# All eight heads in a loop on TensorE and VectorE, wo loaded whole behind V, and a part of the MLP weights on eight DMA engines

## The chip, the cores and the metric

The kernel runs on one core of a Trainium2 chip. All numbers are float32. The metric is device time in microseconds (us) of one execution; the reference point is the median of three runs of the kernel before.

## The reference

One decode step of a gated block, for a batch of 8 with one token each and a model width of 512:

```
xn = layernorm(x)                                    # x: (8, 1, 512)
q  = xn @ wq                                         # 32 query heads of 128
s  = softmax(q k^T / sqrt(128)) v, joined, @ wo      # 8 key/value heads, 4096 positions
z  = gelu(xn @ w_in);  z1, z2 = halves of 896
z2 = layernorm(z2);    g = w_sp * z2 + b_sp          # sequence length 1: two scalars
out = x + s * silu((z1 * g) @ w_out)
```

Every key/value head serves 4 query heads. Each of the two caches holds 8 x 8 x 4096 x 128 numbers, 134 MB. wq and wo are 8 MiB each, w_in and w_out together 5376 KB.

## The kernel before

**Layout and stream.** The host lays out the caches so that, for one head and one half of the batch (4 of 8), the keys or the values are one array of 128 partitions x 16384 columns (8 MiB, `SLOT` columns). SBUF has three such slots, A, B and C. SyncE (SP) issues all large loads, in this order: wq into B, the MLP weights into C, and then for every head h: K's first half into A (called K0 below, `load_k`, L547), K's second half into B (K1), V's first half into C (V0, `load_v`, L553), V's second half into B (V1). Each load waits until TensorE has read what lay in its slot before.

**Compute.** First come the layer norm, the projection of q (`project_q`) and the MLP branch (`mlp`), whose result is the tile `gate`. Then, per head (`head`):

- `spread_q` (L499): VectorE copies the head's q into `qz`, the left operand of the scores.
- `scores` (L506): 32 matmuls per half, q against K, into the PSUM tile `sc`.
- `softmax` (L510 to L529): VectorE takes the maximum, ScalarE the exponential, TensorE and VectorE put sums and maxima of the 4 column groups together and transpose the probabilities.
- `values` (L538 to L541): for each batch entry 8 matmuls with V, then a product and a reduction on VectorE.
- `combine` (L544): a small matmul for each batch entry; the one of entry b stands behind the values of entry b+1.
- L606: VectorE copies the result `po` into `oT`, or, for late heads, into `oT_end`.

Float32 matmuls count as two records each in the profile, transposes as one.

**wo.** There are 32 row blocks m of wo (4 per head), of 128 x 512. Blocks below `FOLDED` (24) are applied in `folded_wo` (L566), 8 output rows in each of four column groups, summed in one PSUM bank; that sum is copied out by VectorE (L620) and put into the final layout by 8 small matmuls (L625). The other blocks go through `direct_wo` (L574), 8 small matmuls each, straight into the final layout. L625 stands between the direct blocks, at `FOLD_AT` (29). Then VectorE multiplies by the gate, adds x (L630, L631), and SP stores the result (L632).

**The last head.** Heads 0 to 6 are a hardware loop on TensorE (`LOOPED`); all other engines' programs, and TensorE's last head, stand singly, instruction behind instruction. In the last head V0 goes into A, 12 blocks of wo (3072 KB) into C, then V1 in two halves of 4096 KB into B, then the other 20 blocks in pieces of 8, 5, 3, 2, 1 and 1 blocks. `folded_wo` of blocks 0 to 11 stands ahead of V1's values, that of 12 to 19 ahead of the last combine, that of 20 to 23 behind it.

**Order and waits.** Nothing is scheduled: the `Recorder` keeps each engine's instructions in the order of the source. `plan` derives the waits from overlapping tile regions and leaves out those that follow from others; `emit_op` writes them. In the loop, TensorE waits for VectorE through a counting semaphore `token`, taken down by one at each use; the large loads have one semaphore for each slot, taken down by 16.

Of the kernel before, what the change touches and what calls it, by code (L numbers as in the profile page):

```python
# [30 lines left out]
WO_EARLY = 12  # L31
WO_LATE = [(WO_EARLY, 20), (20, 25), (25, 28), (28, 30), (30, 31), (31, 32)]
FOLDED = 24
FOLD_AT = 29
LOOPED = HKV - 1
# [44 lines left out]
class Op:  # L80
    def __init__(self, eng, name, args, kw, line):
        self.eng, self.name, self.args, self.kw, self.line = eng, name, args, kw, line
        self.reads, self.writes = [], []
        self.waits = []
        self.sem = None
        self.iter = None
        self.pos = None


class Recorder:  # L90
# [5 lines left out]

    NAMES = ["tensor", "vector", "scalar", "gpsimd", "sync"]

    def __init__(self, nc):
        self.nc = nc  # L100
        self.ops = []
        self.touched = {}
        self.now = None
        self.rounds = 0
        self.order = {n: [] for n in self.NAMES}
        self.dma_sems = {}
        for n in self.NAMES:
            setattr(self, n, Proxy(self, n))
# [8 lines left out]

    def add(self, eng, name, args, kw):
# [5 lines left out]
        op.dma = name == "dma_start"  # L124
        op.key = key
        vals = list(args) + list(kw.values())
        aps = [v for v in vals if isinstance(v, bass.AP)]
# [8 lines left out]
        if eng == "gpsimd" and name == "affine_select":  # L136
            op.reads += op.writes
# [3 lines left out]
        op.at = len(self.order[eng])  # L141
        self.order[eng].append(op)
        op.n = len(self.ops)
        self.ops.append(op)
        op.deps = set()
# [15 lines left out]
    def meet(self, eng):  # L161

        op = Op(eng, "meet", (), {}, 0)
        op.dma, op.key = False, None
        op.deps = {self.order[n][-1] for n in self.NAMES if n != eng and n != "sync" and self.order[n]}
        op.deps = {o for o in op.deps if not o.dma}
        op.at, op.n = len(self.order[eng]), len(self.ops)
        self.order[eng].append(op)
        self.ops.append(op)

    def plan(self):
# [5 lines left out]
        def learn(k, o):  # L177
            for t, v in o.known.items():
                k[t] = max(k.get(t, -1), v)
            k[track(o)] = max(k.get(track(o), -1), o.at)  # L180

        for op in self.ops:
            k = know[op.eng]
            for o in sorted(op.deps, key=lambda o: -o.n):
                if k.get(track(o), -1) < o.at:
                    op.waits.append(o)
                    learn(k, o)
            op.known = dict(k)

        body = [op for op in self.order["tensor"] if op.iter is not None]  # L190
        size = len(body) // self.rounds
        rounds = [body[i * size:(i + 1) * size] for i in range(self.rounds)]
        place = {(o.eng, o.iter, o.pos): o for o in self.ops if o.iter is not None}
        for p in range(size):
            need = set()
            for i, ops in enumerate(rounds):
                assert ops[p].pos == p and ops[p].name == ops[0 * size + p].name
                for o in ops[p].waits:
                    assert o.iter == i, (ops[p].line, ops[p].name, i, o.eng, o.line, o.iter)
                    need.add((o.eng, o.pos))  # L200
            for i, ops in enumerate(rounds):
                ops[p].waits = [place[e, i, q] for e, q in sorted(need)]
        takes = [o.pos for op in rounds[0] for o in op.waits if not o.dma]
        assert takes == sorted(set(takes)), takes
        assert all(o.dma or o.eng == "vector" for op in rounds[0] for o in op.waits)

        for op in self.ops:
            op.token = op.counted = False
        for op in self.ops:
            for o in op.waits:  # L210
                if o.dma:
                    continue
                if op.eng == "tensor" and op.iter is not None:
                    o.token = True
                else:
                    o.counted = True
        for p in range(size):
            any_ = any(ops[p].counted for ops in rounds)
            for ops in rounds:
                ops[p].counted = any_  # L220

        nc = self.nc
        self.first = None
        self.sems = {}

        def sem(name):
            if name not in self.sems:
                self.sems[name] = nc.alloc_semaphore(name)
            return self.sems[name]

        for n in self.NAMES:
            c = 0
            for op in self.order[n]:
                if op.dma:
                    op.sem = sem(op.key or f"dma{op.n}")
                    op.taken = op.key is not None
                    continue
                if op.token and op.counted:
                    c += 1
                elif op.counted:  # L240
                    c += 1
                op.level = c
            sem(n)
        sem("token")

    def emit_op(self, op):
        nc = self.nc
        eng = getattr(nc, op.eng)
        with nc.source_location(__file__, op.line, op.name):
            waits = []  # L250
            for o in sorted(op.waits, key=lambda o: o.n):
                if o.dma:
                    if o.taken:
                        assert op.eng == "tensor"
                        eng.wait_ge(o.sem, 16).then_inc(o.sem, -16)
                    else:
                        waits.append((o.sem, 16))
                elif op.eng == "tensor" and op.iter is not None:
                    t = self.sems["token"]
                    eng.wait_ge(t, 1).then_inc(t, -1)  # L260
                else:
                    waits.append((self.sems[o.eng], o.level))
            for s, v in waits:
                eng.wait_ge(s, v)
# [3 lines left out]
            if op.dma:  # L268
                ins.then_inc(op.sem, 16)
            elif op.counted:  # L270
                ins.then_inc(self.sems[op.eng], 1)
                if op.token:
                    eng.wait_ge(self.sems[op.eng], op.level).then_inc(self.sems["token"], 1)
            elif op.token:
                ins.then_inc(self.sems["token"], 1)

    def emit(self):
        nc = self.nc
        self.plan()
        for n in self.NAMES[1:]:  # L280
            for op in self.order[n]:
                self.emit_op(op)
        ops = self.order["tensor"]
        inside = [i for i, op in enumerate(ops) if op.iter is not None]
        size = len(inside) // self.rounds
        for op in ops[:inside[0]]:
            self.emit_op(op)
        with nc.tensor.Fori(0, self.rounds):
            for op in ops[inside[0]:inside[0] + size]:
                self.emit_op(op)  # L290
        for op in ops[inside[-1] + 1:]:
            self.emit_op(op)
        last = self.ops[-1]
        assert last.dma and last.eng == "sync"
        nc.sync.wait_ge(last.sem, 16)
# [24 lines left out]
def gqa_gmlp_decode(real, x, kT, v, wq, wo, w_mlp, out):  # L320
# [344 lines left out]
```

## Time and profile before

| What | us |
|---|---|
| median of 3 runs (678.53 to 678.9) | 678.71 |
| the profiled execution | 678.71 |
| its span, first to last instruction | 677.3 |
| TensorE matmul busy | 375.2 |
| VectorE busy | 167.5 |
| ScalarE busy | 13.4 |

The profile shows one execution. Times in its rows are us from the start of the span, unless marked ns. PE is TensorE's matmuls, PEld its weight loads, PEldq and PEq its sequencer, DVE is VectorE, ACT ScalarE, SPq the issue queue of SyncE. L538 is line 538 of the kernel before. A row of the timeline has the start, the duration, the engine, the line, the operation, output and inputs, the number of records, and in brackets how long the engine had been idle and what ended that.

### The profile page before, as it was taken

The page shows a single profiled execution, that of the slowest core. Times are in us where ns is not written, and L with a number is a line of the kernel's source. Part 1 is how long each engine was busy: PE and PEld are TensorE (multiplying, and loading weights), DVE is VectorE, ACT ScalarE, POOL GpSimd, SP SyncE. Part 2 cuts the span into 40 slices and gives each one's busy share as a digit, 9 for nine tenths or more (in the row PEclk, how much of TensorE's full clock was granted, in tenths as well). Part 3 has the DMA queues.
Part 4 walks back from the last instruction along what each step waited for, and adds up shares of the span by engine and source line. Part 5 has one row for each costly group of instructions (what it writes and reads, how often), then busy time and mean ns, then how long its engine had stood idle before and what let it go on. Part 6 is the DMA issues. An engine that isn't in the chain of part 4 may idle for free. (4 is left out here: it accounts for less than half of the span.)

```text
span 677.3 us, 5857 instructions
## 1 busy us (share of the span) xinstructions
PE 375.2 (55%) x2658; PEld 119.5 (18%) x2658; DVE 167.5 (25%) x277; ACT 13.4 (2%) x27; POOL 2.8 (0%) x14
## 2 busy tenths in 40 slices
PE   0547554546665455456755454655654465655657
PEld 0122121112111111111211121211211121111212
DVE  2141042302430033401521024401432024400342
ACT  0000000000000000000000000000000000000000
POOL 1000000000000000000000000000000000000000
PEclk9967666878767678877766678887676678766697
DMA  8999999999999999999999999999999999999997
GB/s 373 449 434 434 433 434 433 434 433 433 433 433 433 433 433 433 434 433 433 433 433 433 433 434 433 433 433 437 437 437 437 433 437 445 433 437 434 404 423 318
DMA packets 6233, 290.90 MB, mean 429 GB/s; under 512 B 832, under 2 KB 848, under 8 KB 1360
## 3 DMA queue, kind: packets, MB, share of 16 engines
q1 hardware_dynamic: 6192, 290.75, 99.3%
q8 instruction: 7, 0.11, 0.1%
q10 hardware_dynamic: 32, 0.02, 0.0%
q14 instruction: 2, 0.02, 0.0%
HBM read 290.74 MB, written 0.03 MB: 429 GB/s over the span
## 5 line engine op out<-in xcount | busy, mean ns | idle before, releaser
L506 PE MATMUL sc<-slot_B,qz 128*32 128x512 f32 x512 | 74.4, 746 | 76.6 <-PEq L506 76.6
L538 PE MATMUL o_ps<-slot_B,tbuf 128*16 128x512 f32 x512 | 77.5, 732 | 70.5 <-PEq L538 61.6
L506 PE MATMUL sc<-slot_A,qz 128*32 128x512 f32 x512 | 74.4, 746 | 47.6 <-PEq L506 47.6
L540 DVE TENSOR_TENSOR o_all<-o_ps,diag 128x512 f32<-128x512 f32 x64 | 44.3, 691 | 161.0 <-PE o_ps L538 161.0
L538 PE MATMUL o_ps<-slot_C,tbuf 128*16 128x512 f32 x448 | 67.0, 739 | 20.5 <-PEq L538 20.5
L510 DVE TENSOR_REDUCE nm<-sc 128x1 f32<-128x1024 f32 x8 | 9.8, 1224 | 269.5 <-PE sc L506 269.5
L541 DVE TENSOR_REDUCE o_sb<-o_all 128x128 f32<-128x512 f32 x64 | 67.8, 1060 | 2.2
L506 PEld LDWEIGHTS sc<-slot_B,qz 128*32 128x32 f32 x512 | 20.4, 134 | 130.5 <-issue 130.5
L506 PEld LDWEIGHTS sc<-slot_A,qz 128*32 128x32 f32 x512 | 20.7, 133 | 94.8 <-issue 94.8
L544 PE MATMUL po<-fold,o_sb 128*128 128x4 f32 x128 | 25.6, 270 | 12.3 <-PEq L544 12.3
L544 PEld LDWEIGHTS po<-fold,o_sb 128*128 128x128 f32 x128 | 20.3, 199 | 68.5 <-issue 64.2
L538 PEld LDWEIGHTS o_ps<-slot_B,tbuf 128*16 128x16 f32 x512 | 13.4, 106 | 100.5 <-issue 90.2
L538 PEld LDWEIGHTS o_ps<-slot_C,tbuf 128*16 128x16 f32 x448 | 13.7, 112 | 57.0 <-issue 56.8
L528 PE MATMUL scr<-ident,pbuf 128*128 128x128 f32 x64 | 14.8, 409 | 10.6 <-PEq L528 9.3
L511 ACT ACTIVATE pbuf<-sc,nm 128x1024 f32<-128x1024 f32 x8 | 8.9, 1114 | 556.1 <-DVE nm L510 556.1
L528 PEld LDWEIGHTS scr<-ident,pbuf 128*128 128x128 f32 x64 | 11.8, 211 | 11.0 <-issue 9.7
L529 DVE COPY tbuf<-scr 128x512 f32<-128x512 f32 x16 | 11.1, 692 | 10.6 <-PE scr L528 10.6
L415 PE MATMUL scr<-slot_B,xnT 128*32 128x512 f32 x64 | 9.0, 713 | 8.2 <-PEq L415 8.2
L538 PE MATMUL o_ps<-slot_A,tbuf 128*16 128x512 f32 x64 | 9.8, 753 | 3.9 <-PEq L538 3.9
L514 PE MATMUL scr<-ident,nm 128*1 128x128 f32 x8 | 2.2, 269 | 11.8 <-PEq L514 10.4
L394 PE MATMUL scr<-ident,tbuf 8*128 8x8 f32 x4 | 0.6, 255 | 12.9 <-DVE tbuf L391 12.9
L521 PE MATMUL scr<-wl,same 128*128 128x1 f32 x16 | 3.5, 286 | 6.1 <-PEq L521 5.4
(102 smaller groups left out, 88.4 us busy)
## 6 DMA issues: line engine op xcount, KB each, us to landing
slot_B<-in_v SPq DMA_DIRECT2D x2, 4096.0 KB, 33.8
slot_C<-in_w_mlp SPq DMA_DIRECT2D x1, 5376.0 KB, 34.2
slot_C<-in_wo SPq DMA_DIRECT2D x1, 3072.0 KB, 35.4
slot_C<-in_wo SPq DMA_DIRECT2D x1, 2048.0 KB, 41.4
slot_C<-in_wo SPq DMA_DIRECT2D x1, 1280.0 KB, 44.0
slot_C<-in_wo SPq DMA_DIRECT2D x1, 768.0 KB, 45.4
slot_C<-in_wo SPq DMA_DIRECT2D x1, 512.0 KB, 46.1
slot_C<-in_wo SPq DMA_DIRECT2D x2, 256.0 KB, 46.4
```

What stands on the lines that cost most here:

```text
L415: nc.tensor.matmul(pq[R * g:R * (g + 1), :], xnT[:, k, :], wq_sb[:, k, lo:lo + REP * DH], start=(k == 0), stop=(k == NK - 1))
L506: nc.tensor.matmul(sc[R * g:R * (g + 1), c, :], qz[:, b * R:(b + 1) * R], k_sb[:, i, c, g, :], start=(b == 0), stop=(b == B - 1))
L510: nc.vector.tensor_reduce(nm, sc, op=ALU.max, axis=AX.XY, negate=True)
L511: nc.scalar.activation(p.rearrange("p j s -> p (j s)"), sc.rearrange("p c s -> p (c s)"), AF.Exp, bias=nm, accum_out=l)
L514: nc.tensor.transpose(a, nm, ident)
L521: nc.tensor.matmul(tot, same_all, wl, start=True, stop=True)
L528: nc.tensor.transpose(t[:, j * P:(j + 1) * P], p[:, 4 * c + j, :], ident)
L529: nc.vector.tensor_copy(pT[:, :, 4 * c:4 * c + 4].rearrange("p b j (g r) -> p (j g) b r", g=G), t.rearrange("p (m b r) -> p m b r", b=B, r ...
L538: nc.tensor.matmul(of[R * c:R * c + G * REP, :], pT[:, b, j, :], v_unit[:, j], start=(j < G), stop=(j >= J - G))
L540: nc.vector.tensor_mul(o_all[b % 2], o, diag[:, :, None].to_broadcast([P, G, DH]))
L541: nc.vector.tensor_reduce(o_sb[b % 2], o_all[b % 2].rearrange("p g d -> p d g"), op=ALU.add, axis=AX.X)
L544: nc.tensor.matmul(po[:, b * REP:(b + 1) * REP], o_sb[b % 2], fold, start=True, stop=True)
```

## The change

Five things change together.

- **Loops.** All eight heads, the last one included, are now the loop on TensorE, and VectorE's part of the heads becomes a loop of eight rounds as well. Each pair of an engine and a looping engine gets a semaphore of its own; a wait in the loop is for a fixed count within the round, and at the end of a round the looping engine takes down what the round has counted (`share`): five such waits on TensorE, three on VectorE. An engine outside the loops that waits for an instruction in a loop gets the next later point of that engine at which the instruction is known to be done (`moved`, `early`).
- **Copies.** `spread_q` and the copy of `po` go from VectorE to ScalarE.
- **wo.** In the last head V0 goes into C and V1 into B, in one piece, as in all heads. wo goes into A, where K0 lay, in seven pieces behind V1 (12, 8, 5, 3, 2, 1 and 1 blocks). All its matmuls stand behind the last head.
- **Folding.** 28 blocks instead of 24 are folded, and L625 stands behind block 29.
- **MLP weights.** The last 640 of their 10752 columns are a transfer of their own, `w_low`, whose source has 8 rows instead of 128, so that 8 DMA engines carry it.

The core of the diff:

```diff
-WO_EARLY = 12
-WO_LATE = [(WO_EARLY, 20), (20, 25), (25, 28), (28, 30), (30, 31), (31, 32)]
-FOLDED = 24
-FOLD_AT = 29
-LOOPED = HKV - 1
+WO_PARTS = [(0, 12), (12, 20), (20, 25), (25, 28), (28, 30), (30, 31), (31, 32)]
+FOLDED = 28
+FOLD_AT = 30
+LOW_E = 8
+LOW_COLS = 640
...
+    LOOPS = ["vector", "tensor"]
...
+        moved = {}
         for op in self.ops:
...
+            if self.inside(op):
+                continue
+            for d in op.waits:
+                if d.dma:
                     continue
...
+                at = d
+                if self.inside(d) and d.tokens:
+                    q = d.pos + 1
+                    while any(place[d.eng, i, q].known.get(d.eng, -1) < place[d.eng, i, d.pos].at
+                              for i in all_rounds):
+                        q += 1
+                    at = place[d.eng, d.iter, q]
+                    moved[op.n, d.n] = at
...
+            eng = getattr(nc, n)
+            with eng.Fori(0, self.rounds):
+                for op in ops[first:first + self.size[n]]:
+                    self.emit_op(op)
+                for (m, src), c in sorted(self.share.items()):
+                    if m == n:
+                        s = self.sem(src, n) if src in self.NAMES else self.sem(src)
+                        eng.wait_ge(s, c).then_inc(s, -c)
...
-    nc.sync.dma_start(slots["C"][:, :n_mlp], w_mlp, key="C")
+    n_main = n_mlp - LOW_COLS
+    nc.sync.dma_start(slots["C"][:, :n_main], w_mlp)
+    nc.sync.dma_start(slots["C"][:, n_main:n_mlp],
+                      w_low[:, :P // LOW_E * LOW_COLS].rearrange("e (i n) -> e i n", n=LOW_COLS))
...
-        nc.vector.tensor_copy(qz.rearrange("p (b s) -> p b s", b=B)[:, :, :REP], qT[:, h])
+        nc.scalar.copy(qz.rearrange("p (b s) -> p b s", b=B)[:, :, :REP], qT[:, h])
...
-        nc.sync.dma_start(slots["C"][:, lo * D:hi * D], wo[:, lo * D:hi * D])
-
-    wo_sb = slots["C"].rearrange("p (m d) -> p m d", d=D)
+        nc.sync.dma_start(slots["A"][:, lo * D:hi * D], wo[:, lo * D:hi * D])
+
+    wo_sb = slots["A"].rearrange("p (m d) -> p m d", d=D)
...
     def head(h):
-        last = h == HKV - 1
         spread_q(h)
         for half, n in enumerate("AB"):
             scores(half, load_k(h, half, n))
         softmax()
-        for half, n in enumerate("AB" if last else "CB"):
-            if last and half:
-                load_wo(0, WO_EARLY)
-                v_sb = load_v(h, half, n, 2)
-                for lo, hi in WO_LATE:
-                    load_wo(lo, hi)
-                folded_wo(0, WO_EARLY)
-            else:
-                v_sb = load_v(h, half, n)
+        for half, n in enumerate("CB"):
+            v_sb = load_v(h, half, n)
             for i in range(HALF):
                 b = half * HALF + i
                 values(b, v_sb[:, i])
                 if b > 0:
                     combine(b - 1)
-        if last:
-            folded_wo(WO_EARLY, WO_LATE[0][1])
         combine(B - 1)
...
-        nc.vector.tensor_copy(to, po.rearrange("p (b r) -> p r b", r=REP))
+        nc.scalar.copy(to, po.rearrange("p (b r) -> p r b", r=REP))
...
     nc.meet("tensor")
-    for h in range(LOOPED):
+    nc.meet("vector")
+    for h in range(HKV):
         with nc.round(h):
             head(h)
-    for h in range(LOOPED, HKV):
-        head(h)
-
-    folded_wo(WO_LATE[0][1], FOLDED)
+
+    for lo, hi in WO_PARTS:
+        load_wo(lo, hi)
+    folded_wo(0, FOLDED)
     part_sb = pbuf[:, :D]
     nc.vector.tensor_copy(part_sb, part)
     direct_wo(FOLDED, FOLD_AT)
...
-        "w_mlp": np.concatenate([
...
+        "w_mlp": c(w_mlp[:, :-LOW_COLS]),
+        "w_low": np.concatenate([w_mlp[:, -LOW_COLS:].reshape(LOW_E, -1), np.zeros((LOW_E, 64), np.float32)], axis=1),
```

216 lines of the change are left out of this document (103 added, 113 removed).

## The prediction

> **What bounds the kernel now.** I read the page first: shares, slices, queues.
>
> ```profile
> span 677.3 us, 5857 instructions
> ...
> PE 375.2 (55%) x2658; PEld 119.5 (18%) x2658; DVE 167.5 (25%) x277; ACT 13.4 (2%) x27; POOL 2.8 (0%) x14
> ...
> GB/s 373 449 434 434 433 434 433 434 433 433 433 433 433 433 433 433 434 433 433 433 433 433 433 434 433 433 433 437 437 437 437 433 437 445 433 437 434 404 423 318
> ...
> q1 hardware_dynamic: 6192, 290.75, 99.3%
> q8 instruction: 7, 0.11, 0.1%
> ```
>
> No engine is busy for more than 55%, while the 16 DMA engines are busy for 99.3% of the span and move a flat 433 GB/s. 290.75 MB at that rate take 671.5 us of 677.3. The kernel is one stream of loads; no compute in the middle can gain anything as long as the queue never runs dry. What can move is the start, the evenness of the 16 engines, and what follows the last byte. So the second view is the chain that ended last:
>
> ```profile
> 628.26 46.46 DMA slot_C<-in_wo
> 674.72 0.04 issue
> 674.76 0.47 PE sc L574 x16
> ```
>
> The last piece of wo lands at 674.72, 16 matmul records follow, and TensorE is through at 675.23. From there to the end of the span, 2.07 us, the change touches nothing. Third, the busy time of the DMA engines in the last stretch (the last three figures are granted clock, DMA share and GB/s):
>
> ```profile
> 672.50:673.00 0.50, 0.50 (x48) 0.50 (x44) 0.34 (x1) 0.00 (x0) 0.00 (x0) 1.00 0.55 217
> 673.00:673.50 0.50, 0.49 (x36) 0.33 (x25) 0.35 (x1) 0.00 (x0) 0.00 (x0) 1.00 0.43 168
> 673.50:674.00 0.50, 0.50 (x36) 0.50 (x40) 0.00 (x0) 0.00 (x0) 0.00 (x0) 1.00 0.60 209
> 674.00:674.50 0.50, 0.50 (x44) 0.44 (x32) 0.00 (x0) 0.00 (x0) 0.00 (x0) 1.00 0.14 53
> ```
>
> From 672.5 on about half of the engines have nothing left, and the other half works on for nearly two us. The work left there is (0.55 + 0.43 + 0.60 + 0.14) x 0.5 = 0.86 us of all 16 engines: perfectly even, the stream would end about 1 us earlier. That is the most that evenness is worth.
>
> **The last 640 columns on 8 engines.** The transfer is 128 x 640 x 4 B = 327,680 B: 20,480 B for each of 16 engines, or 40,960 B for each of 8. One engine moves 433/16 = 27.1 GB/s, so 8 engines get 0.76 us more than now and 8 get 0.76 us less, for the rest of the run, as the queue never empties. If the 8 late engines are the relieved ones, every landing from there on comes 0.76 us earlier (the spread of nearly 2 us exceeds twice 0.76); if they are the loaded ones, 0.76 us later. (Its rows are short, 2,560 B; the last wo pieces, with rows of 2,048 B, moved at 217/0.55 = 395 GB/s of all engines, 9% slower, which would make the loaded side 0.9 us, not the one that is then late.) No view names the engines. What makes an engine late is, as I read it, a block of instructions that it has to bring in between loads: the page has 7 of them on q8, 16 KB or about 0.6 us of one engine each. By the start times of the packets they came on engines other than the eight that carry x, and x, of 8 rows like the new transfer, should go to the same eight as that. I take -0.76 us and keep both ends.
>
> **wo whole behind V.** Bytes and order of the rest stay, so the end of the stream stays. But the second half of V now lands before all of wo instead of behind 3072 KB of it, and the 12 matmuls of wo that filled a gap, as well as the 8 between the last units, go behind the last head. So the tail has to be added up again, from these rows (start, us, engine, line, records):
>
> ```profile
> slot_C<-in_wo SPq DMA_DIRECT2D x1, 3072.0 KB, 35.4
> ...
> 191.30 0.18 PEld L538 LDWEIGHTS o_ps<-slot_B,tbuf 128*16 128x16 f32 x8 [8.92 <-issue]
> 204.33 0.36 PE L544 MATMUL po<-fold,o_sb 128*128 128x4 f32 x2 [1.64 <-PEq L544]
> 268.58 0.18 PEld L538 LDWEIGHTS o_ps<-slot_B,tbuf 128*16 128x16 f32 x8 [8.31 <-issue]
> 280.63 0.36 PE L544 MATMUL po<-fold,o_sb 128*128 128x4 f32 x2 [1.64 <-PEq L544]
> ...
> 646.46 2.76 PE L566 MATMUL sc<-slot_C,oT 128*8 128x512 f32 x24
> 662.48 0.15 PEld L538 LDWEIGHTS o_ps<-slot_B,tbuf 128*16 128x16 f32 x8 [5.39 <-DMA slot_B<-in_v]
> 669.40 1.90 PE L566 MATMUL sc<-slot_C,oT 128*8 128x512 f32 x16
> 672.66 0.69 DVE L620 COPY pbuf<-sc 128x512 f32<-128x512 f32 x1 [0.81 <-PE sc L566]
> 673.69 0.30 PEld L625 LDWEIGHTS sc<-pbuf,same 128*32 128x32 f32 x16
> 673.97 0.63 PE L574 MATMUL sc<-slot_C,oT_end 128*32 128x64 f32 x32
> ```
>
> - V complete: TensorE now starts on V's last piece at 662.48, when it has landed. Without 3072 KB (3.15 MB, 7.26 us at 433 GB/s) ahead of it that is 655.22, with the relieved engines 654.46.
> - The last half head, from that start to the start of the last combine (L544): 13.03 us in head 1 and 12.05 in head 2, the ends of what the heads show; they differ by when the granted clock goes from 0.5 to 1.0 after the wait for V. I take the middle, 12.54: 667.00.
> - Leaving the loop: 0.5 us, next paragraph: the first wo matmul at 667.5.
> - 28 folded matmuls are 56 records. 24 took 2.76 us and 16 took 1.90, so eight more cost 0.86: 2.76 + 4 x 0.86 = 6.2 us, until 673.7. All pieces they need land earlier: behind rows 0 to 27 only 4 rows, 1 MB or 2.4 us of stream, are left, so they are there by about 671.5.
> - Copy of the sum on VectorE: 0.69, and about 0.1 us for the handover on each side (an estimate: the wo load above was handed over in 0.04): 674.6. The 32 records of rows 28 and 29 run meanwhile (0.63).
> - L625 and the last 32 records: 673.69 to 674.60 here, 0.91 us. TensorE is through at 675.5.
>
> The stream's own end would be 674.72 - 0.76 = 673.96, and with 0.51 for the 16 records behind it 674.47. So TensorE, not the stream, is now last by 1 us: before, the stream was last, and TensorE had almost no idle time left in front of it. Against 675.23 that is +0.27 us.
>
> **The two loops.** TensorE's last head joins the loop; what the head computes is the same. New at the loop's end are five waits that take back the round's counts, in front of the increment and the branch:
>
> ```profile
> L288 PEldq COMPARE_BRANCH  x7: 76/208/228, 126.6 to 590.6; - x7
> ...
> L574 PEldq EVENT_SEMAPHORE  x1: 51/51/51, 673.1 to 673.1; - x1
> ```
>
> With the increment priced like a wait, 6 x 51 + 76 to 228 ns are 0.38 to 0.53 us behind the issue of the last combine, part of it beside that matmul (0.36): I take 0.5 us from the combine's start to the first fold. Seven times it lies between heads, where TensorE waits for K anyway; the eighth is on the path, and is in the sum above. VectorE gets three such waits and a branch a round; between heads it has nothing to do from its last copy, over at 591.18, until K's scores, which are at work until after 607 (rows below), and at the last exit its next work is 6 us off. Both programs shrink (VectorE's 277 instructions and TensorE's last head stood singly), so a few instruction blocks go, at up to 0.6 us on one engine each. Other late engines remain, so I count 0, and one block, 0.6 us gain, for the low end.
>
> [...] TensorE's loop branched seven times (six back, one out). The queues of 420 to 590 us, a stretch with two of the returns, list no instruction packet; this is the only line:
>
> ```profile
> q1 hardware_dynamic: 1269, 73.73, 100.1%
> ```
>
> [...]
>
> **Copies on ScalarE.** Nearest rows, and the path between heads:
>
> ```profile
> L519 ACT ACTIVATE w<-w 128x1 f32<-128x1 f32 x8 | 1.6, 203 | 2.7 <-DVE w L518 2.7
> 588.61 0.33 SPq L547 DMA_DIRECT2D slot_B<-in_kT  x1
> 589.34 1.02 DVE L541 TENSOR_REDUCE o_sb<-o_all 128x128 f32<-128x512 f32 x1
> 590.90 0.19 DVE L606 COPY oT_end<-po 128x32 f32<-128x32 f32 x1 [0.54 <-PE po L544]
> 591.01 0.17 DVE L499 COPY qz<-qT 128x32 f32<-128x32 f32 x1
> 597.31 9.95 PE L506 MATMUL sc<-slot_A,qz 128*32 128x512 f32 x64 [6.45 <-PEq L506]
> ```
>
> A small ACT operation takes 0.20 us against 0.19 and 0.17: both ready by 591.4 instead of 591.2, and K0 is first read at 597.31. Hidden with 5.9 us to spare; without that cover 0.2 us a head. After the last head the oT copy is due only 6.2 us later. Price 0.
>
> **SP's waits.** The waits for freed slots move to a later instruction of TensorE: K1's load goes out when the last combine may start (590.36, the end of the reduction) instead of at 588.61; V's second waits for the maximum as well, one VectorE operation. Queued behind each is the next load. At 590.4 the stream still has K0 to bring, which TensorE gets at 597.3, and 6.9 us cover the 2.4 us or so that the whole start of the stream costs (first slice: 373 of 433 GB/s over 16.9 us). The extra transfer at the start is issued ahead of K0, whose turn in the stream comes only behind both weight transfers. Price 0; it would turn into a loss, eight times over, only with 4.5 us more delay.
>
> **Sum.** The profiled execution took 678.71 us, equal to the median of the runs shown, 1.41 beyond its span. +0.27 gives 678.98: I predict 679.0 us. A measurement tells about 0.2%, 1.36 us, from no change: faster means under 677.35, slower over 680.07.
>
> **Rivals.**
> 1. Leaving the loop makes TensorE wait for its next instructions. For: the old exit lay under the idle time of 6.45 us in front of the 597.31 row, so that much would not have shown, and it now stands on the path. Against: no instruction packets around the loop's returns. Half of that, 3.2 us, gives 682.2, slower; it decides from 1.1 us on. As the trace speaks against it, 0.1. [...]
> 2. The late engines are the ones loaded more. V then lands at 655.22 + 0.76, 1.52 us later than forecast: 680.5, slower. Or the transfer spreads over all 16 and nothing shifts: V at 655.22, 679.7. For both only that no view names engines. 0.12.
> 3. The tail on TensorE is a us shorter, because the clock is up sooner (the head 2 row: -0.5) and fewer instruction packets delay V: then the stream ends the kernel, 678.71 - 0.76 = 677.95, or 677.35 with the 0.6. 0.25, on the border of a measurable gain.
> 4. The clock is late instead (head 1's row, +0.48, and what lies beyond these seven heads): 679.5 to 680.1. 0.13. The forecast itself, 678.5 to 679.5: 0.4.
>
> **How the numbers follow.** 80% reach from 677.3 (the third rival's low end) to 680.7, which takes in the second rival; the stall at the exit (0.1) and the far ends are left out. Faster by over 0.2% needs the third rival and more evenness than the 0.76 us: 0.12. Slower: rival 1, most of rival 2 and half of the fourth: 0.26. Within 0.2%: 0.62.
>
> **What would show it.** In the profile after: wo's last piece landing near 674.0 and the DMA share in the last two us falling at once instead of in two steps (evenness); the chain that ended last going back through L620's copy and the folded matmuls instead of a wo load (TensorE last); V's second half begun near 654.5 and its last combine 12 to 13 us later; the first folded matmul 0.5 us behind it, any gap over 1 us being the first rival; no slice under 430 GB/s in the middle. If the chain still ends in a wo load, the tail's sum is wrong; if TensorE idles inside it, the loop's exit is.

## The result, and the profile after

| | before | after |
|---|---|---|
| median, us | 678.81 (678.45 to 679.01, 6 runs) | 683.12 (682.83 to 684.04, 6 runs) |
| the profiled execution, us | 678.71 | 683.79 |
| its span, us | 677.3 | 682.5 |

The change makes the kernel slower: the ratio of the times is 1.0067, with a 95% interval of 1.0054 to 1.008. Forecast were 679.0 us and a range up to 680.7.

The page of the changed kernel first: its span, the queue of the loads and a queue of instruction blocks.

```profile
span 682.5 us, 5725 instructions
...
q1 hardware_dynamic: 6184, 290.75, 98.7%
q8 instruction: 5, 0.08, 0.0%
```

The stream brings the same 290.75 MB, and two instruction blocks fewer. The stream's bytes are not the reason. The chain that ended last, in the profile after:

```profile
669.97 0.36 issue
670.33 7.93 PE sc L580 x56
678.26 0.02 issue
678.29 0.70 DVE pbuf L625
...
```

It goes back through the copy of the sum (L625) and the 28 folded blocks (L580) and no longer ends in a load of wo: TensorE is last, as forecast. But the chain's long piece takes 7.93 us where 6.2 were forecast, and it starts at 670.33 instead of 667.5. Where that comes from is in the timeline after (start, duration, engine, line, operation, in brackets the idle time and what ended it):

```profile
657.22 3.62 PE L555 MATMUL o_ps<-slot_B,tbuf 128*16 128x512 f32 x16 [8.19 <-DMA slot_B<-in_v]
...
668.09 1.02 DVE L558 TENSOR_REDUCE o_sb<-o_all 128x128 f32<-128x512 f32 x1
669.26 0.36 PE L561 MATMUL po<-fold,o_sb 128*128 128x4 f32 x2 [1.64 <-DVE o_sb L558]
669.65 0.19 ACT L610 COPY oT_end<-po 128x32 f32<-128x32 f32 x1 [38.64 <-PE po L561]
670.33 7.89 PE L580 MATMUL sc<-slot_A,oT 128*8 128x512 f32 x56 [0.72 <-PEq L304]
...
679.28 0.63 PE L588 MATMUL sc<-slot_A,oT_end 128*32 128x64 f32 x32
```

Read against the prediction's tail, row by row:

| step | forecast | measured | difference |
|---|---|---|---|
| V's last piece begun | 654.46 | 657.22 | +2.76 |
| from there to the last combine | 12.54 | 12.04 | -0.50 |
| last combine to first folded matmul | 0.5 | 1.07 | +0.57 |
| 28 folded blocks | 6.2 | 7.93 | +1.73 |
| from there until TensorE is through | 1.8 | 1.65 | -0.15 |
| TensorE is through at | 675.5 | 679.91 | +4.41 |
| from there to the end of the span | 2.07 | 2.59 | +0.52 |

Three steps failed, and a small one at the end. The first is late data, so the last stretch of the stream comes next (the last three figures are granted clock, DMA share and GB/s):

```profile
672.50:673.00 0.50, 0.50 (x6) 0.00 (x0) 0.00 (x0) 0.00 (x0) 0.00 (x0) 0.50 1.01 406
673.00:673.50 0.50, 0.50 (x8) 0.19 (x4) 0.00 (x0) 0.00 (x0) 0.00 (x0) 0.50 0.81 324
673.50:674.00 0.50, 0.50 (x5) 0.02 (x1) 0.00 (x0) 0.00 (x0) 0.00 (x0) 0.50 0.68 266
674.00:674.50 0.50, 0.50 (x8) 0.16 (x4) 0.00 (x0) 0.00 (x0) 0.00 (x0) 0.64 0.66 258
674.50:675.00 0.50, 0.50 (x8) 0.12 (x4) 0.00 (x0) 0.00 (x0) 0.00 (x0) 1.00 0.44 172
```

The share should have fallen at once. It falls in more steps than before and is still 0.44 from 674.5 on, where the kernel before had nothing left to start (0.00): the engines have become less even, not more. The same rows show the second surprise: until about 674.4 the granted clock is 0.50, right in the middle of the folded blocks.

### The profile page after: what moved, and what is told of

Its sections match the earlier page's. It is cut to its first block, busy times and chain, and to the rows that moved or that the text cites. A ratio compares the mean times of both kernels' runs of the same rounds, so it can differ in the third digit from the quotient of the medians.

```text
span 682.5 us, 5725 instructions
## 1 busy us (share of the span) xinstructions
PE 370.8 (54%) x2602; PEld 115.7 (17%) x2602; DVE 165.2 (24%) x261; ACT 15.0 (2%) x43; POOL 2.7 (0%) x14
## 3 DMA queue, kind: packets, MB, share of 16 engines
q1 hardware_dynamic: 6184, 290.75, 98.7%
## 5 line engine op out<-in xcount | busy, mean ns | idle before, releaser
L523 PE MATMUL sc<-slot_B,qz 128*32 128x512 f32 x512 | 72.7, 732 | 81.1 <-DMA slot_B<-in_kT 81.1
L523 PE MATMUL sc<-slot_A,qz 128*32 128x512 f32 x512 | 72.1, 726 | 48.3 <-DMA slot_A<-in_kT 46.4
L555 PE MATMUL o_ps<-slot_C,tbuf 128*16 128x512 f32 x512 | 76.5, 739 | 27.5 <-DMA slot_C<-in_v 27.5
L523 PEld LDWEIGHTS sc<-slot_B,qz 128*32 128x32 f32 x512 | 17.7, 132 | 136.1 <-DMA slot_B<-in_kT 88.4
L561 PE MATMUL po<-fold,o_sb 128*128 128x4 f32 x128 | 25.4, 269 | 13.6 <-DVE o_sb L558 13.5
L555 PEld LDWEIGHTS o_ps<-slot_C,tbuf 128*16 128x16 f32 x512 | 15.6, 112 | 69.5 <-issue 69.2
L580 PE MATMUL sc<-slot_A,oT 128*8 128x512 f32 x56 | 7.9, 726 | 0.7 <-PEq L304 0.7
```

Of the source, the lines that this page charges most:

```text
L523: nc.tensor.matmul(sc[R * g:R * (g + 1), c, :], qz[:, b * R:(b + 1) * R], k_sb[:, i, c, g, :], start=(b == 0), stop=(b == B - 1))
L555: nc.tensor.matmul(of[R * c:R * c + G * REP, :], pT[:, b, j, :], v_unit[:, j], start=(j < G), stop=(j >= J - G))
L561: nc.tensor.matmul(po[:, b * REP:(b + 1) * REP], o_sb[b % 2], fold, start=True, stop=True)
L580: nc.tensor.matmul(part[R * r:R * r + B, :], oT[:, h, r, :], wo_sb[:, m, :], start=(m < REP), stop=(m >= FOLDED - REP))
```

## The experiments

The theory after this reading had three parts: the 8-engine transfer delays the landings by 2 us instead of saving 0.76; the exit from TensorE's loop costs twice its price; and the idle time at the exit makes the clock drop, at 1.7 us. The rivals: the late landings come from the new place of wo or from the loops; the slow folding comes from something in the folding itself. Line numbers differ a little from kernel to kernel. Each kernel has one profiled execution, and a folding row with fewer than 56 records is one at which the view shown ended.

### The 8-engine transfer: taken out, put in alone, and spread over 16

`a_no_low` is the change with the MLP weights in one transfer again:

```diff
-    nc.sync.dma_start(slots["C"][:, :n_main], w_mlp)
-    nc.sync.dma_start(slots["C"][:, n_main:n_mlp],
-                      w_low[:, :P // LOW_E * LOW_COLS].rearrange("e (i n) -> e i n", n=LOW_COLS))
+    nc.sync.dma_start(slots["C"][:, :n_mlp], w_mlp)
```

> The changed kernel with the MLP weights in one transfer on 16 engines again; all else as changed. Theory 1 (the transfer on 8 engines delays the whole stream by about 2 us): V's last piece is begun near 655 us instead of 657.2, and the kernel takes 680.5 to 681.7 us instead of 683.1. Rival (V is late for another reason, SP's later waits or the loops): V's last piece still at 657, 683 us.

`b_before_low` is the kernel before with nothing but this transfer (the diff above the other way round).

> The kernel before with nothing changed but the last 640 MLP columns as a transfer on 8 engines. Theory 1: the last piece of wo lands 1.5 to 2.5 us later, near 676.7, and the kernel takes 680.3 to 681.3 us. The prediction's step (late engines relieved): 0.76 us earlier, 678.0. Rival of the prediction (late engines loaded, nothing else): 679.5.

`c_low16` is the change with `LOW_E = 16`: the same extra transfer with its short rows, from 16 source rows. That 16 engines carry it is the author's reading; no view shows how many did.

> The changed kernel with the same 640 columns as the same extra transfer, but from 16 source rows, so on 16 engines. If what costs is that 8 engines carry it, this is like one whole transfer: V's last piece near 655, 680.5 to 681.7 us. If the short rows of 2,560 B or the extra transfer as such cost: V's last piece near 657, 683 us.

Measured: `a_no_low` 681.10 us (680.23 to 682.18), ratio to the kernel before 1.0041 (1.0027 to 1.0055); `b_before_low` 680.96, ratio 1.0035 (1.0022 to 1.0047); `c_low16` 681.71, ratio 1.0044 (1.0027 to 1.0061). Without the transfer the changed kernel gains 2.0 us, and alone the transfer costs the kernel before about 2.4 (0.0035 x 678.6). From the timeline of `a_no_low`, the start of V's last piece, and from the chain of waits of `b_before_low`, the last load:

```profile
654.97 3.61 PE L552 MATMUL o_ps<-slot_B,tbuf 128*16 128x512 f32 x16 [8.99 <-DMA slot_B<-in_v]
```

```profile
631.61 45.59 DMA slot_C<-in_wo
```

V's last piece begins 2.25 us earlier without the transfer (654.97 against 657.22), near the 655.22 that the prediction had without any shift between engines. In the kernel before, which the stream ends, the last piece of wo lands at 677.20 (631.61 + 45.59) instead of 674.72 once the transfer is in. In `c_low16`, with 16 source rows, V begins at 655.52; its time is no better than that of `a_no_low`, whose folding ran at full clock in its profile while this one's ran at half clock, below. So it is the 8 source rows that cost, and with them the 8 engines (about as many are at work on `w_low` in the trace, below). The extra transfer with its short rows makes at most 0.55 us of it (655.52 against 654.97, one execution each), and the loops and the new place of wo have no part in it: the transfer alone costs the kernel before 2.48 us at its last landing.

### Where the bytes of the 8 engines go

That 8 engines carry 20,480 B more each explains at most 0.76 us (at 27.1 GB/s for one engine). Two more kernels are the kernel before with an additional transfer of 320 KB from 8 source rows, into columns of C that nothing reads, once into partitions 0 to 31 and once into 64 to 95 (the computation is unchanged, the work is additional):

```diff
+    nc.sync.dma_start(slots["C"][LOW_AT:LOW_AT + 32, n_mlp:n_mlp + 2560],
+                      w_low[:, :4 * 2560].rearrange("e (i n) -> e i n", n=2560))
```

> The kernel before with an extra transfer that nobody reads, as many bytes as the 640 columns (320 KB), from 8 source rows, so on 8 engines, into partitions 0 to 31 behind the MLP weights. Theory (the 8-engine transfer costs twice because it writes rows that the other engines also write): here only the 8 carrying engines are late, by 1.5 us; the other engines bring K at full rate meanwhile and half of them have nothing left from about 672.8 on; 680 us or so, as the latest of the carrying engines ends 1.5 us later. Rival (8 engines on a transfer of their own slow all): all 16 late by 1.5 us or more.

> [...] Theory: both groups are late, the carrying engines by 1.5 to 3 us, the others by 0.7 to 1.5 us; no engine has run dry before 673.5; 680.5 to 682 us. Rival (the destination rows do not matter): the same as with partitions 0 to 31.

Measured: 680.05 us for the low partitions, ratio 1.0021 (1.0011 to 1.0031), and 681.50 for the high ones, ratio 1.0043 (1.0028 to 1.0058). The last load in the chain of waits (start, duration), low first, high second:

```profile
630.22 46.12 DMA slot_C<-in_wo
...
676.39 0.47 PE sc L580 x16
```

```profile
631.53 46.06 DMA slot_C<-in_wo
...
677.63 0.47 PE sc L580 x16
```

The load ends at 676.35 and at 677.59, against 674.72 in the kernel before. Low rows cost 676.35 - 674.72 = 1.63 us, about what 40,960 B at 27.1 GB/s, 1.51 us, cost an engine that was among the last already. The expectation that half of the engines would have nothing left from 672.8 on was not met: the DMA share is 0.84 and 0.87 in the two half us from 673.0, against 0.43 and 0.60 in the kernel before. So the latest engine seems to be among the eight, but hardly all of the eight were late. The same bytes into high rows cost 2.87 us. So 1.24 us depend on nothing but the rows that are written. In stretches of half a us, first from the kernel with low rows, then from the one with high rows:

```profile
35.50:36.00 0.50, 0.37 (x4) 0.13 (x2) 0.09 (x1) 0.00 (x0) 0.00 (x0) 1.00 0.43 184
```

```profile
35.50:36.00 0.50, 0.00 (x0) 0.00 (x0) 0.44 (x1) 0.00 (x0) 0.00 (x0) 1.00 0.58 123
36.00:36.50 0.50, 0.47 (x12) 0.44 (x15) 0.00 (x0) 0.00 (x0) 0.00 (x0) 1.00 0.50 102
36.50:37.00 0.50, 0.50 (x14) 0.35 (x9) 0.00 (x0) 0.00 (x0) 0.00 (x0) 0.83 0.68 193
```

These shares count a packet where it starts, so large packets give bursts and zeros, and each row is read as the ratio of bytes to busy time. With low rows 184 GB/s go with a share of 0.43: 428 GB/s at full share, the usual rate (the whole stream's is 433). With high rows 123 go with 0.58 and 102 with 0.50: 212 and 204 GB/s at full share, half. (The third row, 284, lies between the two rates.) The changed kernel has the same half rate while `w_low` moves, which goes into all 128 partitions:

```profile
35.00:35.50 0.50, 0.00 (x0) 0.00 (x0) 0.46 (x1) 0.00 (x0) 0.00 (x0) 1.00 0.52 108
35.50:36.00 0.50, 0.33 (x9) 0.36 (x13) 0.02 (x1) 0.00 (x0) 0.00 (x0) 1.00 0.54 113
```

These rows give 208 and 209 GB/s at full share. Their shares, 0.52 and 0.54, are 8.3 and 8.6 of the 16 engines: about eight were at work on the transfer. An estimate from them: at half rate, 13.5 GB/s, the 40,960 B of one engine take 3.0 us, 2.3 us more than the 20,480 B at full rate in one whole transfer. That is near the 2.25 us of V and the 2.48 of the last landing. A transfer on few engines is thus not only a matter of which engine has how many bytes: its rate also depends on the rows that it writes (428 GB/s at full share into the low ones, 204 to 212 into the high ones). That other engines fill the same rows at the same time, the theory in the expectations, was the author's assumption and was not shown: no view names the engine of a packet or the rows it writes, and the runs show only the difference between the rows.

### The exit and the clock: other work in the gap

`d_filler` is the change with four matmuls into an unread part of PSUM ahead of every head's last combine, where TensorE otherwise waits for VectorE. `e_no_low_filler` is `a_no_low` with the same.

```diff
+        for g in range(G):
+            nc.tensor.matmul(scr[2][R * g:R * (g + 1), :], same_all[:, :R], pbuf[:, :BANK], start=True, stop=True)
         combine(B - 1)
```

> The changed kernel with 4 more matmuls (8 records, result unused) ahead of each head's last combine, where TensorE waits for the last reduction. Clock theory (TensorE's clock halves in the folding because the window before it had too little work): the 56 folded records take 6.2 us instead of 7.9, the kernel 681.4 to 682. Rival (the clock falls after some 10 us of full speed whatever TensorE does): 7.9 us again, 683 us.

> The changed kernel with the MLP weights in one transfer, and with the 4 filling matmuls ahead of each last combine. Clock theory: the runs without filler fell into two groups, near 680.2 and near 682.1, by whether the clock halves for one stretch of 3.4 us in the tail; with work in that gap all runs are near 680.2 to 680.6. Rival (the halving comes whatever TensorE does): two groups again, median near 681.

Measured: `d_filler` 682.24 us, ratio 1.0052 (1.0035 to 1.0069); `e_no_low_filler` 680.93 (680.16 to 681.44), ratio 1.0035 (1.0022 to 1.0049). With filler the changed kernel's folding takes 6.19 us instead of 7.89, with V's last piece begun at nearly the same time (657.16). Here are the stretches of 3.41 us before and during the fall of the clock (the first figures are the length and TensorE's busy time): first of the changed kernel, then of `c_low16`, then of `a_no_low` and last of `d_filler`.

```profile
667.54:670.95 3.41, 1.05 (x11) 0.54 (x14) 1.54 (x2) 0.19 (x1) 0.00 (x0) 1.00 0.99 420
670.95:674.37 3.42, 3.42 (x20) 0.74 (x16) 0.00 (x0) 0.00 (x0) 0.00 (x0) 0.50 0.89 359
```

```profile
665.29:668.70 3.41, 1.09 (x12) 0.69 (x12) 1.71 (x2) 0.18 (x1) 0.00 (x0) 1.00 0.96 408
668.70:672.12 3.42, 3.42 (x20) 0.77 (x16) 0.00 (x0) 0.00 (x0) 0.00 (x0) 0.50 1.00 411
```

```profile
666.86:670.27 3.41, 1.92 (x18) 0.77 (x22) 0.67 (x1) 0.18 (x1) 0.00 (x0) 1.00 0.98 411
670.27:673.68 3.41, 3.41 (x36) 0.93 (x32) 0.00 (x0) 0.00 (x0) 0.00 (x0) 1.00 0.84 335
```

```profile
668.70:672.12 3.42, 2.07 (x22) 0.73 (x22) 0.88 (x1) 0.19 (x1) 0.00 (x0) 1.00 0.99 415
```

After a stretch in which TensorE is busy for 1.05 or 1.09 of 3.41 us, 31 to 32%, the next one is granted exactly half; after 1.92 or 2.07 us, 56 to 61%, the clock stays up. Two waits make the idle time: 1.64 us for VectorE ahead of the last combine and 0.72 at the loop's exit. `a_no_low` has the same two waits; there the boundary at 666.86 (an estimate: the last change of its clock, at 660.0, and two stretches of 3.41 us) falls into the first of them (666.04 to 667.68) and the clock stays up in the profiled execution, which would explain why its executions lie up to 2 us apart. In `d_filler` the boundaries lie elsewhere as well (668.70 by the same estimate, from 661.9): only 0.35 us of the filling matmuls (667.99 to 669.05) are in the stretch shown, and without them about 1.7 us, half of it, would still have been work. So its profile alone doesn't separate the filler from the place of the boundary. Its times agree with the theory: all four executions (682.02 to 682.78) are below the fastest of the changed kernel (682.83), though above the 681.4 to 682 expected. For `e_no_low_filler` no execution came near 682, but they spread to 681.44 where 680.2 to 680.6 were expected, and the median isn't clearly below that of `a_no_low`: on the time alone this pair decides nothing.

`k_wider_gap` is `a_no_low` with VectorE's last product of each head done four times over (the repeated product changes nothing in the result), so that the wait is about 2.1 us longer and no place of a boundary saves the clock:

```diff
-            nc.vector.tensor_mul(o_all[b % 2], o, diag[:, :, None].to_broadcast([P, G, DH]))
+            for _ in range(4 if b == B - 1 else 1):
+                nc.vector.tensor_mul(o_all[b % 2], o, diag[:, :, None].to_broadcast([P, G, DH]))
```

> The changed kernel with the MLP weights in one transfer, and with VectorE's last product of each head made four times, so that TensorE waits 2.1 us longer for the last reduction. Clock theory (a stretch of 3.41 us with under about 0.45 of it at work halves the clock for the next one): the stretch with the wait is now always that empty, so the folding, 6.2 or 7.9 us by chance without it, takes 7.9 us in the profile, and all runs lie near 682.3 + 1.7 = 684 us, without the group at 680.2. Rival (the halving has another cause): both groups again, moved by 2.1 us, 682.3 and 684.2.

Measured: 685.30 us (684.35 to 686.13), ratio 1.0101 (1.0084 to 1.0117): 4.2 us more than `a_no_low`, twice the added work, and its folding takes 9.03 us where 7.9 were expected. The stretches, cut where the clock changes:

```profile
666.09:669.51 3.42, 0.00 (x0) 0.00 (x0) 3.27 (x5) 0.00 (x0) 0.00 (x0) 1.00 0.98 414
669.51:672.92 3.41, 2.80 (x14) 0.96 (x18) 0.00 (x0) 0.19 (x1) 0.00 (x0) 0.50 1.00 406
672.92:676.33 3.41, 3.41 (x20) 0.66 (x16) 0.00 (x0) 0.00 (x0) 0.00 (x0) 0.50 0.17 64
```

The wait now fills a whole stretch, and half clock follows it, as expected; but it lasts for two stretches and not for one, though TensorE is busy for 2.80 of 3.41 us in the first of them. With the second stretch the folding takes 1.1 us more than expected, and the theory as written did not have it. In the changed kernel and in `c_low16` the clock came back after a single stretch, which was busy throughout. All executions lie 2 us or more above the slowest of `a_no_low`, none in its range. The fall after too little work is thus borne out; the rule by which the clock comes back stays open. What the traces show of the stretches is their length and their boundaries. In the changed kernel the clock is at half from 653.89 to 660.71, at full to 670.95 and at half to 674.37: 6.82, 10.24 and 3.42 us, or two, three and one times 3.41. From kernel to kernel the boundaries lie elsewhere (667.54, 665.29 and 666.86 above). And 31% busy was already too little.

### The tail order without the loops

`f_before_tail` is the kernel before with wo behind V into A, 28 folded blocks and `FOLD_AT` 30, and nothing else of the change.

> The kernel before with only the last head's order of the change: V's second half in one piece behind V's first, wo whole behind it in K0's slot, 28 blocks folded behind the last head. No loop is changed, q and oT copies stay. Theory: V's last piece begun near 655.1, 0.3 to 0.4 us from last combine to folding instead of 1.07, folding 6.2 or 7.9 us by the clock: 679.4 to 681.2 us, some 0.7 us under the whole change without the 8-engine transfer. Rival (the tail's order is free and the loops cost): 678.7.

Measured: 679.21 us (678.88 to 680.9, 10 runs), ratio 1.0013 (1.0003 to 1.0022). From its timeline:

```profile
655.14 3.61 PE L537 MATMUL o_ps<-slot_B,tbuf 128*16 128x512 f32 x16 [9.11 <-PEq L537]
667.56 0.39 PE L543 MATMUL po<-fold,o_sb 128*128 128x4 f32 x2 [1.55 <-DVE o_sb L540]
667.87 6.20 PE L565 MATMUL sc<-slot_A,oT 128*8 128x512 f32 x56
```

V at 655.14 (655.22 forecast without a shift), 12.42 us to the last combine (12.54), folding 6.20 (6.2), and no gap: 0.31 us, one matmul's length. The prediction's tail sum holds, and TensorE is last. Two of the ten executions, 680.28 and 680.9, lie 1.1 and 1.7 us above the profiled one, 679.19; whether the clock fell in them, without any wait at an exit, no trace shows.

### Which loop

`g_tensor_loop_only` and `h_vector_loop_only` are `a_no_low` with only one of the two loops; the other engine's program stands singly, all eight heads.

```diff
-    LOOPS = ["vector", "tensor"]
+    LOOPS = ["tensor"]      # in h: ["vector"]
```

> The change without the 8-engine transfer, and with the loop of eight heads on TensorE alone; VectorE's program stands singly. Theory: all of the exit's price is TensorE's (its waits on the round's counts, the increment and the branch). Then the first folded matmul starts 0.8 to 1.1 us after the start of the last combine, and the output store takes about 1.8 us, because the instruction block that TensorE fetches behind its loop falls beside it; about 680.3, and 1.7 us more (682.0) in the executions in which the granted clock falls to 0.5 at the start of the folding. Rival: VectorE's loop exit also delays something at the end; then this kernel is nearer to 679.2, the time of the tail order alone, with a gap of 0.3 us.

> The change without the 8-engine transfer, and with the loop of eight heads on VectorE alone; TensorE's program stands singly, all eight heads. Theory: no exit on TensorE, so the first folded matmul starts 0.3 us after the start of the last combine, the clock stays at 1.0, folding takes 6.2 us in every execution, and the output store about 1.5 us: 679.2, as with the tail order alone, unless TensorE's longer program brings more instruction blocks into the stream of loads, which could add up to 0.6 us. Rival: VectorE's loop exit delays the last product or the copies behind it; then the idle time ahead of the folding, or of the copy of the sum, is over 1 us here too, and the time is 680 to 682.

Measured: 680.95 us (680.33 to 681.73), ratio 1.0034 (1.0021 to 1.0047), with TensorE's loop alone; 681.85 (681.65 to 682.48), ratio 1.0048 (1.003 to 1.0066), with VectorE's alone. The second was expected at 679.2. From the two timelines, `g_tensor_loop_only` first:

```profile
666.95 0.38 PE L558 MATMUL po<-fold,o_sb 128*128 128x4 f32 x2 [1.55 <-DVE o_sb L555]
...
667.93 4.02 PE L577 MATMUL sc<-slot_A,oT 128*8 128x512 f32 x20 [0.60 <-PEq L304]
...
665.02:668.44 3.42, 1.27 (x16) 0.79 (x16) 1.71 (x2) 0.18 (x1) 0.00 (x0) 1.00 1.00 422
```

```profile
q8 instruction: 20, 0.33, 0.2%
...
657.83 3.61 PE L552 MATMUL o_ps<-slot_B,tbuf 128*16 128x512 f32 x16 [9.15 <-PEq L552]
...
670.39 0.38 PE L558 MATMUL po<-fold,o_sb 128*128 128x4 f32 x2 [1.55 <-DVE o_sb L555]
670.70 1.88 PE L577 MATMUL sc<-slot_A,oT 128*8 128x512 f32 x13
```

TensorE's loop alone has the whole gap, 0.98 us; VectorE's alone has none, 0.31. The exit's price is TensorE's. The last row shown of `g_tensor_loop_only` is the stretch before its folding: 1.27 us busy, 37%, and the clock fell here too (the whole folding took 7.89 us). That execution took 681.21 us, where 682.0 was expected of one like it. What makes `h_vector_loop_only` slow lies elsewhere: TensorE's program without a loop brings 20 instruction blocks into the stream instead of 5, and V begins 2.86 us later than in `a_no_low`. My expectation allowed 0.6 us for that. That blocks of instructions make single engines late is how the prediction read the unevenness; this run agrees with it, though it shows the sum of fifteen blocks and not one, and no view shows on which engines they came.

### The exit's instructions

The last run asks what the gap is made of. From the rows of TensorE's sequencer in the changed kernel (count, then ns of one as least, median and most, then the first and the last start in us):

```profile
L304 PEldq EVENT_SEMAPHORE  x40: 51/51/51, 129.1 to 669.9; - x40
...
L298 PEldq ALU_OP  x8: 36/36/42, 129.9 to 670.1; - x8
L298 PEldq COMPARE_BRANCH  x8: 76/208/226, 130.0 to 670.2; - x8
```

A wait is recorded with 51 ns. But in the first round the first of five starts at 129.1 and the increment behind them at 129.9: 0.16 us from start to start. At the exit the last wait starts at 669.9, the increment at 670.1, the branch at 670.2 and the folding at 670.33. Seven steps of about 0.15 us make 1.05, the whole gap of 1.07. `l_early_take` is `a_no_low` with each count taken down by the round's last wait on that semaphore, so that nothing but the increment and the branch is left behind the last combine:

```diff
-                    eng.wait_ge(s, self.rank[op.eng, d.eng, d.pos])
+                    c = self.rank[op.eng, d.eng, d.pos]
+                    w = eng.wait_ge(s, c)
+                    if c == self.share[op.eng, d.key if d.dma else d.eng]:
+                        w.then_inc(s, -c)
...
-                for (m, src), c in sorted(self.share.items()):
-                    if m == n:
-                        ...
-                        eng.wait_ge(s, c).then_inc(s, -c)
```

> The change without the 8-engine transfer, and with the round's counts taken down by the last wait of the round on each semaphore itself, instead of by five waits of their own behind the last combine (three on VectorE); both loops still have eight rounds. Theory: each of the seven instructions behind the last combine (five waits, increment, branch) takes about 0.15 us from start to start, though its record is 36 to 76 ns long, and that, not a fetch of instructions, is the whole gap of 1.0 us. With two of the seven left, partly beside the last combine, the first folded matmul starts 0.3 to 0.45 us behind that combine's start; TensorE's idle time ahead of the folding falls by 0.6 us, so the granted clock stays at 1.0 and folding takes 6.2 us in every execution: 679.3 to 680.0, and no execution near 682. Rival 1: the gap is the price of leaving the loop as such (fetching the instructions behind the branch); then it stays at 0.8 us or more and the time at 681. Rival 2: the gap goes, but the clock still falls in some executions; then the median lies between 679.7 and 681.5, with single executions 1.7 us above the others.

Measured: 680.70 us (679.51 to 681.09), ratio 1.0031 (1.0019 to 1.0043). From its timeline:

```profile
666.33 1.02 DVE L554 TENSOR_REDUCE o_sb<-o_all 128x128 f32<-128x512 f32 x1
667.65 0.35 PE L557 MATMUL po<-fold,o_sb 128*128 128x4 f32 x2 [2.02 <-PEq L557]
667.93 5.34 PE L576 MATMUL sc<-slot_A,oT 128*8 128x512 f32 x48
```

The gap is 0.28 us with both loops still there: it was the five waits, not the branch or a fetch behind it. The gain in time fell short of the 679.3 to 680.0 expected. In part that is because the last combine now starts 0.30 us after the reduction ends (667.35) instead of 0.15 (669.11 to 669.26 in the changed kernel): from the reduction's end to the first folded matmul 0.58 us instead of 1.22. No execution is near 682, yet the median isn't clearly better than that of `a_no_low`: the profiled execution, with a folding of 6.20 us, is the best of six and the others lie up to 1.6 us above it. These are the times of the second rival, by which the clock still falls in some executions, and TensorE's idle time ahead of the folding did fall only from 1.64 + 0.68 = 2.32 us in `a_no_low` to 2.02. What the executions differ in stays open all the same, since only one of each kernel has a trace.

No run beats the kernel before. Nearest is `f_before_tail`, at 1.0013.

## Why the prediction was wrong

- **"The last 640 columns on 8 engines"** failed, in sign and in size: -0.76 us was taken and +2.2 measured (657.22 against 654.97). The step reasoned only on bytes per engine at full rate, and guessed that the eight engines of x, and so of the new transfer, were not the late ones, from start times of packets, which name no engine. The low-rows run fits a latest engine among the eight (+1.6 us for 1.5 us of bytes). The half rate was in none of its bounds: even the second rival, +0.76, reached only 655.98 for V.
- **"Leaving the loop: 0.5 us"** was mis-sized by half: 1.07. The mechanism, waits and branch on the path, was right, but they were priced by the length of their records, 51 ns, and not by the time from start to start, about 150 ns. The first rival, a fetch of instructions, is excluded by `l_early_take`; its deciding point of 1.1 us was nearly reached by another cause.
- **"28 folded matmuls: 6.2 us"** holds at full clock (6.20 in `f_before_tail` and `a_no_low`) and failed at half clock: 7.89. The prediction let the clock enter only behind the wait for V, as its fourth rival; that TensorE's idle time just ahead of the folding, 1.64 us before the last combine and 0.72 at the exit, would bring the clock down again isn't in it. If the wait at the exit tipped it, these 0.7 us cost 2.4; no pair of traces with the same boundaries shows that.
- **V begun to last combine**: 12.54 forecast, 12.04 measured and 12.42 in `f_before_tail`, at the low end of the rows and between their ends. The rows of two heads were not the ends of what can come: `c_low16` took 11.77. That TensorE and not the stream would be last was right, and so was the rest of the tail sum: `f_before_tail` came to 679.21.
- **"From there to the end, the change touches nothing"**: 0.5 us too short. The output's issue rows of before and after:

```profile
out<-res SPq DMA_DIRECT2D x1, 32.0 KB, 1.5
```

```profile
out<-res SPq DMA_DIRECT2D x1, 32.0 KB, 1.9
```

  The store takes 1.4 to 1.5 us in all six kernels with seven or no rounds in TensorE's loop, and 1.6 to 2.2 us in all eight with eight rounds. In the latter one instruction block is fetched about when the result is stored (in the changed kernel at 680.0, with the store issued at 680.49); that this is the cause is argued, not shown.
- **Copies on ScalarE** and **SP's waits**, price 0: right. The copy of `po` takes 0.19 us (the 669.65 row above) and nobody waits for it; between 37 and 600 us the stream moves 434 GB/s:

```profile
37.00:600.00 563.00, 307.03 (x2077) 94.97 (x2075) 138.76 (x205) 12.23 (x38) 0.57 (x1) 0.75 1.00 434
```

Together +2.76 - 0.50 + 0.57 + 1.73 - 0.15 + 0.52 = 4.93 us on the profiled execution, and its span is 4.9 us above the 677.57 forecast. The three failures meet on one path: moving all of wo behind the last head put TensorE last, and the exit and the clock then count in full. Late data counts either way, as `b_before_low` shows.

## What to carry to other kernels

- Price a chain of sequencer instructions by the time from one start to the next (about 0.15 us here), taken from the first and last starts of their rows, not by the length of their records (51 ns); and put the bookkeeping of a hardware loop ahead of its last useful instruction (here the gap at the exit fell to 0.28 us by that).
- Before moving bytes between DMA engines, ask which engines are late and into which rows the bytes go (1.63 us into the low rows and 2.87 into the high ones here); one run of the transfer alone shows its price.
- On a path that TensorE ends, add up its idle time over any 3.4 us: two short waits in one such stretch, 1.64 and 0.72 us here, can halve the clock for the work behind them.

## What the runs showed of the hardware

- 320 KB from 8 source rows cost 1.63 us at the end of the stream when written to partitions 0 to 31, and 2.87 us to partitions 64 to 95, beside a full stream.
- Semaphore waits behind one another on TensorE's sequencer start about 0.15 us apart (five from 129.1 to 129.9), three times their recorded 51 ns.
- TensorE's clock was halved for a stretch of 3.4 us after one such stretch at 31 to 37% busy, and not after one at 56 to 61%; what lies between was not measured. After a stretch without any work it stayed at half for two.
- With fifteen more instruction blocks of 16 KB V began 2.86 us later, five times their share of the stream (0.25 MB at 433 GB/s are 0.58 us).
